# Batch 1's attention beside batch 0's second dense layer: another order of the same steps

## The chip, the cores and the metric

The kernel runs on one core of a Trainium2 chip. The metric is device time in microseconds (us) of one execution; lower is better. The engines are TensorE (PE, with PEld its weight loads), VectorE (DVE), ScalarE (ACT), GpSimd (POOL) and SyncE (SP, which here only issues transfers). Each engine works through a queue of its own in order; between engines, semaphores hold an instruction back until its inputs and its buffer are there.

## The reference

Four batches of eight heads, 768 tokens, head size 64. Attention sees the first 4 tokens (sinks) and a window of 128 tokens back; the result goes through two dense layers with a squared ReLU between them.

```python
scores = scale * np.matmul(q, k.transpose(0, 1, 3, 2))
keep = is_sink | in_window          # pos < 4, or 0 <= rel < 128
scores = np.where(keep, scores, -1000000000.0)
...
a = np.exp(scores - max); a = a / (sum(a) + 1e-09)
attn_out = np.matmul(a, v)
x = attn_out.transpose(0, 2, 1, 3).reshape(B * S, H * D)   # 3072 x 512
h = x @ w_in                                               # 512 x 2048
r = np.maximum(h, 0.0); g = r * r
out = g @ w_out                                            # 2048 x 512
```

## The kernel before

All work is cut into 992 numbered steps (`Op`), built in the code in a fixed numbering. A step is a handful of instructions on one engine: a load, a set of transposes, one pair of score tiles, one exponential, one mask, one product of a dense layer, one copy out of PSUM, one store. A batch of 768 tokens is worked on in three token blocks of 256 (s or u = 0, 1, 2). Of the heads, m counts four pairs; a score step takes two pairs in batches 1 to 3.

The order of everything is one hand-kept string, `ORDER`. `Plan.run` walks through its words. A word is a step's number, a letter for the engine where there is a choice (p, d, a, g for PE, DVE, ACT, POOL; without a letter the first engine in the step's table), and `+0` or `+1` for the pool of PSUM that it takes its buffer from. The steps are issued in that order, so the string sets, for each engine, the order of its queue, and with it the buffers: a buffer is handed on when the last reader's word has been passed, first freed, first taken:

```python
            for s in o.takes:
                if len(s.pools) > 1:
                    s.pool = s.pools[int(chosen.pop(0))]
                s.room = free[s.pool].pop(0)
            ...
            o.run(o.engine)
            for s in o.reads:
                s.readers -= 1
                if not s.readers:
                    free[s.pool].append(s.room)
```

PSUM has four such buffers of two banks: two in the pool `att`, two in `den`. Transposes, scores, values and both dense layers all take from these four, so most PE steps wait for the ACT or DVE step that empties the buffer they get.

The stages that meet in the changed stretch, with the step numbers that the text uses:

- Loads of batch 1: POOL issues q and k (37 to 44, 49 to 52; L371; 40 is the last of the first four of k, 44 the last of the first four of q), v (45 to 48, 53, 54; L380). The transfers cast to bf16. Loads of batch 2: 444 to 461 (L402, L414). 87 builds the mask constants on POOL (L257 to L259).
- Batch 0, first dense layer, third token block: products 184, 193, 187, 190 (L762, 16 matmuls of 256 columns each); their ReLU (185, 194, 188, 191; L776 on ACT, L778 on DVE) and squares (186, 195, 189, 192; L785, L787).
- Batch 0, second dense layer: first block 282 to 289 (L990) with copies 290, 291 on ACT and the store 292 (L1013); second block 297 to 308 and third 316 to 327, seven products each by sums and differences of blocks (L1239), their sums on DVE (L1213) and their copies and additions (L192, L194, L1253), stores 311 and 330 (L1282).
- Batch 1, transposes of k (200, 196, 204, 208) and q (201, 197, 205, 209) in one PE step per pair of heads (L503, four matmuls), 252 and 255 for the last two tiles; each is copied out by 198, 199, 202, 203, 206, 207, 210, 211, 253 to 257.
- Batch 1, attention: scores 216, 223 (block 0), 234, 241 (block 1), 260, 267 (block 2) on PE (L609); exponentials 217, 219, 224, 226, 235, 237, 242, 244, 261, 263, 268, 270 on ACT (L630); masks on DVE (L639, L642) or POOL (L218); sink keys 213, sink scores 214 and 258 (L568), sink values 212 (L550); values 221, 228, 239, 246, 265, 272 (L678); normalizing (L694, L695); transposes of the result, "bridges", 230, 232, 248, 250, 274, 276 (L727).
- Batch 1, first dense layer: blocks 0 and 1 together, 343 to 406, in four groups of seven products (L892) with copies `t` (L192, L194), bounded sums `r` (L942), ReLU (L967, L969) and squares (L915, L917); block 2 from 412, behind a spread copy 407 on ACT.
- Batch 2 begins: SP turns its q and k by transposing transfers (462 to 473, L460), sink keys 475, scores 485 and 478 with exponentials 486, 488, 479, 481 and masks 487, 489.
- 530 is the first product of batch 1's second dense layer.

Before the changed stretch the queues of both kernels are the same, and behind 490 they are again.

Of the kernel before, what the change touches and what calls it, by code (L numbers as in the profile page):

```python
# [18 lines left out]


ORDER = """
990 1 0 2 7 8 9 10 11 12 13 14 15 16 17 18 56d 60a 55d 991+0 3 19 57+0 61d 20 5 6 4 62+1 65 59a 67+0 58a 21 64d 89d
63a 68+0 75+1 88d 69 70 76+1 22 71+0 77 23 72 73 78 24 94a 79+1 90+0 93d 92a 95+1 80 91d 81 96a 74 100+0 82 101+0 25
26 102 83+1 97d 66 84d 27 104 85 110+1 111+0 103g 86d 152+1 112 28 113d 105d 98+0 99 153 106+0 108 114 115d 154a 116+1
118 29 160+1 109 161 162a 107 30 119 117 120+0 31 155d 163a 122 121d 123d 32 168+0 156+1 331 33 172+0 157 169 164+1
170a 165 34 35 158d 173 166a 124+1 125a 127+0 36 159d 176+1 129a 177 126d 174a 140+1 133+1 37 128d 171d 142 136 180+1
181 282+0 38 178d 167d 137d 132+0 141+1 182a 130+0 39 283 40 144 143d 41 134 42 43 332 284 285 131 145d 146+0 175a 147
135g 278 179a 286 138+1 139 287 288 148+0 150 334 151d 44 149a 279 183d 289 184+1 290 185 193+0 280 281 200+0 201 291
194 45 204+1 196+0 202 46 203 205 198a 186 197 207a 293 206 187+0 199a 216+0+0 47 48 195a 217 49 188d 234+1+0 50 235
190+0 219 208+0 87 292 237 209 295 191 218 297+0 189 220 51 336 52 212 53 210a 294 211 255+0 252+1 254 299 298 256 54  # L30
253a 257 444 223+0+1 333 238d 445 192a 226 304 213 224 221+0 312 222 300 241+1+0 301 214+0 296 244 215 302 225 446
303d 242 306 260+0+0 236 462 263 307 314 337 316+0 245d 243d 315 227 308 313 447 318 319 464 246+0 261 247 239+0 448
240 320 321 228+0 475 322d 317 229 258+0 335 259 325 449 450 310 326 230+0 451 231 452 232 248+0 233 249a 327 250 251a
323 309 305 343+1 359+1 339 338 344 467 340 345 341 360 463 329 311 453 324 328 346 465 347 361 362 363 267+1+1 348
349 350 364 268 342 365d 270 351d 366 367 375+0 352 376 377 354 368 454 355 468 356d 370 369a 357 455 391+0 456 379
264 457 262 466 458 265+0 271 393 353 459 378 269 371 392 395 358a 266 372 272+0 373 381 380 382 474 374a 397 394 273
274+0 383d 276 277 396 275a 384 469 407 386 485+0+0 388d 718 472 387 470 460 486 398 410 461 408 389 412+1 488 471
478+1+0 409 399 473 385 479 400 487 330 413 688 402 414 428+0 404 401 403 405 430 416 429 418 432 406a 489 530+0 481
415 390 417 431 419 532 689 526 411 490+0 434 420 433 435 528 421 423 491 436 437 707 482 527 422a 533 424 480 534 690
708 476+0 477 425 439 440 441 691 535 442 531 483+1 426 529 484 443a 536 494+0+0 537 438a 497 692 427 495 568+0 545  # L40
539 540 570 564 566 492 693 694 695 542 498d 501+0+0 502 565 696 541 493 571 504 697 706 538 572 698 543 569 709
517+0+1 518 546 699 573 544 547 520 700 575 503d 510+0+0 701 574 549+0 496d 583 711 576 567 577 584 578 521d 513 505
579 585 551 581 506+0 552 580 507 514 511 586 512d 553 519 713 588+0 499+0 710 500 554 702 703 555d 515+0 516 522+0
589 719 550 590 712 523 591 745+0+0 748 592 558 556 548 560 746 738+0+0 741 594d 557 593 587 595 559 562 739 561
722+0+0 747 596d 714 604+0 749d 725 597 606 599 605 600 726 601 608 607 715 508 509 723 602 524 716 525 717 656+1 657
598 720+0 658 609 620 721 659 610 622 640+0 750+0 724 611 642 612 621 641 751 613 742 603a 660 662 740 615 644 623 646
614 727+0 616 704 661 617 663 563 643 645 618 647 619 672+0 664 667 665 648 651 649 728 582 674 668 673 669 650 676
670 743+0 652 666a 675 744 653 624+1 678 671a 677 654 626 679 625 729+1+0 680 730 628 770 681 655 630 683 774+0 771
732 684 627 775 685 686 629 772 776 754+0+1 682a 755 731 631 777 687 733 773 632 734+0 735 778 635 779 757 705 761+1+0
633 637 636 781 752 758 780d 634 762 638 756 639a 736 793+0 783 789 764 790 784 759+0 737 791 785 795 760 763 782 765  # L50
794 827 828 800 832+1 766+0 786 787 767 848+0 788 850d 829 833 808 796 834 835 830 849 797 768 836 838d 810 851 753
798 837 852 812+1 792 839 853 799 854 855 856 769 801 802 804 840d 859 803 841 857 831 814 843 815 858 842a 866 844
861 805d 816 845 811 809 806 860 817 868+0 813 862 864 846 819 865 818 863 869 870 884+1 867 871 821 872 885 874 823
886d 873 875 822 847 876 916+0 824 887 888 917 889 932 825 877 878 879 890 934 820 918 880 919 920 900+1 807 902 881d
882 933 891 921 883a 901 892 904 936+0 922d 938 906 903 923 905 893 924d 895 896 907 925 894a 897 939 935 908d 927 898
928 926a 940 929 937 826 911 909 899a 913 910 930 941 931 912 942 914 943 946 915 970 955+1 944 945 957 951 974+0 948
953 971 947 952 958 975 949 959d 956 972 960 950 961 973 977+0 962 976 978 964 954 966 979d 965 963 980 968 981 982
985 967d 969 983 984 989 986 988 987
"""
# [1350 lines left out]
```

## Time and profile before

| | |
|---|---|
| median of 3 runs | 210.15 us (209.98 to 210.62) |
| profiled execution | 209.26 us, of which 207.6 us span |
| granted TensorE clock | 1.0 |
| busy: PE, PEld, DVE, ACT, POOL | 199.6, 176.2, 174.7, 133.9, 96.2 us |

The span runs from the first to the last instruction of the program. A window row shows a stretch's length, then for each engine the us in which it was busy and the number of instructions, then clock, DMA share in engines' tenths, GB/s. A timeline row shows start, length, engine, line, operation, what is written from what, and how many instructions were merged; in square brackets the idle time before it and what ended it. A matmul's shown length includes its way through the array, so PE's pace is read from start to start.

### The profile page before, as it was taken

What the parts mean: (1) busy time and instruction counts of PE and PEld (TensorE: products, weight loads), DVE (VectorE), ACT (ScalarE), POOL (GpSimd) and SP (SyncE); (2) the same over time, 40 slices, a digit from 0 to 9 for tenths busy, and PEclk for the clock granted to TensorE, in tenths of its full rate; (3) what the DMA queues carried; (4) which work ended last, traced back from release to release, by engine and by line L of the source; (5) the groups of instructions that cost most, each with busy time, mean ns of one, the idle gap of its engine ahead of it and who ended that gap; (6) DMA issues with size and microseconds to landing.
All of it is one profiled execution on the core that took longest, in us unless ns stands there. A gap on an engine that the chain in (4) does not pass through costs nothing.

```text
span 207.6 us, 6021 instructions
## 1 busy us (share of the span) xinstructions
PE 199.6 (96%) x2500; PEld 176.2 (85%) x2502; DVE 174.7 (84%) x342; ACT 133.9 (64%) x208; POOL 96.2 (46%) x137
## 2 busy tenths in 40 slices
PE   7969999999899999999999999999999999999993
PEld 7458997579878899889878988998889999999893
DVE  4387657498899998999998778999989998998853
ACT  2769458729998168898888458989871452584010
POOL 7799275699499927999333529000280000000000
PEclk9999999999999999999999999999999999999999
DMA  5999999999999999999999996901023220200205
GB/s 157 220 218 200 186 185 212 180 156 175 159 75 126 147 129 225 117 182 155 123 142 235 103 135 194 115 3 25 12 42 129 53 94 10 104 0 0 104 0 202
DMA packets 96042, 26.10 MB, mean 126 GB/s; under 512 B 86800, under 2 KB 93456, under 8 KB 96016
## 3 DMA queue, kind: packets, MB, share of 16 engines
q0 software_dynamic: 69248, 12.59, 86.5%
q1 hardware_dynamic: 25568, 12.49, 27.2%
q10 hardware_dynamic: 1200, 0.66, 1.1%
q8 instruction: 19, 0.31, 0.6%
q14 instruction: 7, 0.06, 0.1%
HBM read 27.30 MB, written 6.29 MB: 162 GB/s over the span
## 4 chain that ended last, share of the span: by engine, by line
PE 80%; DVE 6%; ACT 6%; DMA 4%; issue 2%; POOL 0%; ACTq 0%; POOLq 0%; DVEq 0%
PE py L1239 28%; PE pm L892 25%; PE pm L762 9%; PE po L678 6%; PE ps L609 4%; DMA v<-in_v_dram 4%; PE py L990 3%; ACT expm L630 2%; PE py L1100 2%; PE pt L503 1%; DVE r L942 1%; ACT gT_sb L915 1%; PE px L727 1%; DVE xn_sb L695 1%; ACT qkT L192 1%
## 5 line engine op out<-in xcount | busy, mean ns | idle before, releaser
L630 ACT ACTIVATE expm<-ps 128x1024 bf16<-128x1024 f32 (+1 forms) x48 | 43.8, 951 | 9.6 <-PE ps L609 7.6
L218 POOL TENSOR_SCALAR_AFFINE_SELECT expm<-expm 128x512 bf16<-128x512 bf16 x34 | 24.0, 740 | 42.2 <-DVE xn_sb L695 19.5
L942 DVE CUSTOM_DVE_ANT_0 r<-pm,t 128x512 bf16<-128x512 f32 x54 | 36.0, 684 | 1.6 <-PE pm L892 1.2
L1239 PEld LDWEIGHTS <-gT_sb 128*128 128x128 bf16 x320 | 30.4, 98 | 4.4 <-issue 0.6
L892 PEld LDWEIGHTS <-w_in_sb 128*128 128x128 bf16 x384 | 32.4, 114 | 1.7 <-issue 1.5
L192 ACT ACTIVATE t<-pm 128x512 f32<-128x512 f32 x42 | 24.7, 600 | 13.4 <-PE pm L892 12.7
L892 PEld LDWEIGHTS <-wi 128*128 128x128 bf16 x288 | 24.7, 114 | 0.8 <-issue 0.7
L1239 PEld LDWEIGHTS <-sg 128*128 128x128 bf16 x240 | 22.5, 98 | 3.1 <-DVE sg L1213 0.3
L192 ACT ACTIVATE osb<-py 128x256 f32<-128x256 f32 (+1 forms) x36 | 14.1, 397 | 15.7 <-PE py L1239 15.0
L762 PE MATMUL pm<-xT,w_in_sb 128*128 128x256 bf16 x192 | 22.5, 273 | 0.1
L892 PE MATMUL pm<-xs,wi 128*128 128x256 bf16 (+1 forms) x192 | 21.6, 246 | 0.0
L892 PE MATMUL pm<-xs,w_in_sb 128*128 128x256 bf16 (+1 forms) x192 | 21.5, 246 | 0.0
L762 PEld LDWEIGHTS <-w_in_sb 128*128 128x128 bf16 x192 | 20.5, 114 | 0.8 <-issue 0.5
L1239 PE MATMUL py<-wt,gT_sb 128*128 128x256 bf16 x160 | 20.7, 273 | 0.2
L1239 PE MATMUL py<-wt,sg 128*128 128x256 bf16 x160 | 20.8, 273 | 0.0
L1239 PE MATMUL py<-w_out_sb,gT_sb 128*128 128x256 bf16 x160 | 20.4, 273 | 0.0
L915 ACT ACTIVATE gT_sb<-r 128x1024 bf16<-128x1024 bf16 x17 | 18.0, 1056 | 1.8 <-DVE r L942 1.6
L678 PE MATMUL po<-v,expm 128*128 128x65 bf16 x352 | 17.9, 193 | 1.1 <-DMA v<-in_v_dram 1.1
L678 PEld LDWEIGHTS <-expm 128*128 128x128 bf16 x352 | 16.8, 97 | 2.3 <-issue 1.3
L695 DVE TENSOR_TENSOR xn_sb<-po,rc 128x512 bf16<-128x512 f32 (+1 forms) x28 | 17.2, 615 | 1.0
L1253 DVE TENSOR_TENSOR osb<-py,osb 128x256 f32<-128x256 f32 x30 | 12.1, 416 | 4.7 <-PE py L1239 4.6
L609 PE MATMUL ps<-qkT 64*128 64x128 bf16 (+1 forms) x256 | 14.5, 238 | 1.1 <-ACT expm L630 0.6
(107 smaller groups left out, 377.8 us busy)
## 6 DMA issues: line engine op xcount, KB each, us to landing
out_dram<-osb SPq DMA_DIRECT2D x11, 512.0 KB, 3.0
v<-in_v_dram POOLq DMA_DIRECT2D x24, 128.0 KB, 7.0
qn<-in_k_dram POOLq DMA_DIRECT2D x20, 128.0 KB, 6.6
qn<-in_q_dram POOLq DMA_DIRECT2D x20, 128.0 KB, 6.3
w_in_sb<-in_moe_w_in_dram POOLq DMA_DIRECT2D x4, 512.0 KB, 9.2
w_out_sb<-in_moe_w_out_dram POOLq DMA_DIRECT2D x4, 512.0 KB, 10.5
qr<-in_k_dram SPq DMA_DIRECT2D x4, 256.0 KB, 6.9
qr<-in_q_dram ACTq DMA_DIRECT2D x2, 256.0 KB, 4.2
```

The costliest lines, as they stand in the source:

```text
L192: return nc.scalar.activation(out=dst, in_=src, func=AF.Copy)
L218: nc.gpsimd.affine_select(out=e_tile, in_=e_tile, compare_op=ALU.is_ge, fill=fill, base=i - 1, pattern=[[0, n], [1 if i else -1, 128]], ch ...
L609: nc.tensor.matmul(ps[:, h2, o:o + w], lhsT=qkT_sb[r, m, 1, c, :], rhs=qkT_sb[r, m, 0, qb:qb + w // 128, :], start=(i == 0 and not biased) ...
L630: nc.scalar.activation(out=x[:, :, o:512], in_=bank_t["s", b, s, m][:, :, o:512], func=AF.Exp, scale=scale)
L678: touch(("po", b, s, m0), e, nc.tensor.matmul(pv[:, i, h2, :], lhsT=lhsT, rhs=rhs, start=(n_ == 0), stop=(n_ == len(mms) - 1)), j)
L695: touch(("po", b, s, m0), e, nc.vector.tensor_tensor(out=xn_sb[:, 2 * s:2 * s + 2, 128 * (m0 + j0):128 * (m0 + j0 + nj)].rearrange("p i (j ...
L762: nc.tensor.matmul(pm[:, i, :], lhsT=w_in_sb[:, fb // 4, kb, fb % 4:512:4], rhs=xT[:, c0 // 256:(c0 + cw) // 256, kb, :], start=(kb == 0), ...
L892: touch(tag, e, nc.tensor.matmul(y[:, bk, i, :], lhsT=weights(name, f0 + i, a), rhs=rhs[:, a, :], start=fresh and i == 0 and a == 0, stop= ...
L915: nc.scalar.activation(out=d, in_=x, func=AF.Square)
L942: touch(tag, e, nc.vector._custom_dve(TENSOR_ADD_SAT, out=d.rearrange("p n c -> p (n c)"), in0=T["y"][:, 1].rearrange("p n c -> p (n c)"), ...
L1239: touch((b, u), e, nc.tensor.matmul(region(name), lhsT=x[:, i, :], rhs=w_[:, i, :], start=first and i == 0, stop=i == HB - 1, skip_group_c ...
L1253: ins = nc.vector.tensor_tensor(out=d, in0=region(of), in1=d, op=ALU.add)
```

## The change

The word order in `ORDER` is changed between the 188th and the 476th of the 992 words. Outside that stretch the words stand where they stood. Many words gain an engine letter; for nearly all that letter names the engine which the word without it meant. 28 steps do run on another engine: 14 from DVE to ACT (copies 206, 211, 254, 257, 303, 322, 233, 365; squares 189, 353, 390, 401; ReLU 356, 388), 10 from ACT to DVE (copies 199, 207, 253, 309, 361, 367; ReLU 191; squares 192, 369, 406), masks 236 and 262 and the sink values 212 from POOL to DVE, mask 238 from DVE to POOL. In eight words the PSUM pool is another one. The start of the stretch:

```diff
-278 179a 286 138+1 139 287 288 148+0 150 334 151d 44 149a 279 183d 289 184+1 290 185 193+0 280 281 200+0 201 291
-194 45 204+1 196+0 202 46 203 205 198a 186 197 207a 293 206 187+0 199a 216+0+0 47 48 195a 217 49 188d 234+1+0 50 235
-190+0 219 208+0 87 292 237 209 295 191 218 297+0 189 220 51 336 52 212 53 210a 294 211 255+0 252+1 254 299 298 256 54
-253a 257 444 223+0+1 333 238d 445 192a 226 304 213 224 221+0 312 222 300 241+1+0 301 214+0 296 244 215 302 225 446
-303d 242 306 260+0+0 236 462 263 307 314 337 316+0 245d 243d 315 227 308 313 447 318 319 464 246+0 261 247 239+0 448
+147d 135g 278d 179a 286 138+1 139d 287 288 148+0 150 334d
+151d 44g 149a 279d 183d 289 290a 200+0 280d 291a 45g 196+0 184+0 46g 201 87g 197 212d 185a 198a 193+0 47g 48g 202d
+203d 293d 204+0 205 186d 49g 194a 187+0 295d 50g 206a 199d 207d 195a 216+0+0 217a 234+1+0 219a 237a 188d 51g 296d
+208+1 235a 209 292 336d 210a 211a 52g 53g 190+1 297+0 281d 220d 189a 255+0 213a 294d 299a 236d 191d 252+1 254a 257a
+54g 238g 298 253d 256d 444g 304 218d 192d 223+0+1 305d 462 445g 224a 214+0 215a 300 226a 221+0 446g 301a 333d 312d
+222d 241+0+1 302 242a 260+0+0 447g 313d 227d 448g 465 303a 261a 306d 244a 307 314d 308 230+0 309d 225d 310d 316+0
...
```

and its end, from batch 1's last bridges on:

```diff
-274+0 383d 276 277 396 275a 384 469 407 386 485+0+0 388d 718 472 387 470 460 486 398 410 461 408 389 412+1 488 471
-478+1+0 409 399 473 385 479 400 487 330 413 688 402 414 428+0 404 401 403 405 430 416 429 418 432 406a 489 530+0 481
...
+275a 396 398 485+0+0 386 407a 399a 486a 718g 461g 311 384d 402 388a 385d 470 400d 487d 387 389d 404a 403 405d 488a
+412+1 428+0 471 688g 429 414a 410d 408d 401a 478+1+0 689g 430a 413 409d 411d 406d 415d 479a 481a 472 416 418a 432 390a
+530+0 489d 473 330 434a 417 419 431d 420a 526d 532a 490+0 433 435 528d 421d 423 491d 436a 437d 707 482d 527d 422a 533
...
```

TensorE's queue in the stretch, by step numbers, before:

```
184 193 200 201 204 196 205 197 187 216 234 190 208 209 297 255 252 298 223 304 221 300 241 214 302 260 307 316
308 319 246 239 321 228 317 258 326 230 232 248 327 250 323 343 359 344 360 347 363 267 348 350 364 366 375 376
354 355 370 391 379 265 371 392 395 272 380 382 274 276 396 386 485 387 398 412 478 413 402 428 403 416 429 432 530
```

and after:

```
200 196 184 201 197 193 204 205 187 216 234 208 209 190 297 255 252 298 304 223 214 300 221 241 302 260 307 308
230 316 228 239 319 246 232 248 321 250 317 258 359 343 344 360 323 347 326 327 363 348 350 267 364 366 354 375
355 370 371 391 265 392 272 376 379 274 395 276 380 382 396 398 485 386 402 387 403 412 428 429 478 413 416 432 530
```

POOL issues step 87 ahead of 47 instead of behind 50, and the 16 loads 444 to 459 one after another, ahead of masks 264, 269 and 271. SP turns in the order 462, 465, 463, 464, 467, 466, 469, 468, then the store 311, where it stood behind the fourth turn before.

More of the change, by code (lines that the diff above doesn't have):

```diff
@@ L21 @@
 ORDER = """
[L22 to L26, printed above, removed]
@@ L27 @@
-181 282+0 38 178d 167d 137d 132+0 141+1 182a 130+0 39 283 40 144 143d 41 134 42 43 332 284 285 131 145d 146+0 175a 147
-135g 278 179a 286 138+1 139 287 288 148+0 150 334 151d 44 149a 279 183d 289 184+1 290 185 193+0 280 281 200+0 201 291
-194 45 204+1 196+0 202 46 203 205 198a 186 197 207a 293 206 187+0 199a 216+0+0 47 48 195a 217 49 188d 234+1+0 50 235
-190+0 219 208+0 87 292 237 209 295 191 218 297+0 189 220 51 336 52 212 53 210a 294 211 255+0 252+1 254 299 298 256 54
-253a 257 444 223+0+1 333 238d 445 192a 226 304 213 224 221+0 312 222 300 241+1+0 301 214+0 296 244 215 302 225 446
@@ L32 @@
-303d 242 306 260+0+0 236 462 263 307 314 337 316+0 245d 243d 315 227 308 313 447 318 319 464 246+0 261 247 239+0 448
[L33 to L36, printed above, removed]
@@ L37 @@
-274+0 383d 276 277 396 275a 384 469 407 386 485+0+0 388d 718 472 387 470 460 486 398 410 461 408 389 412+1 488 471
-478+1+0 409 399 473 385 479 400 487 330 413 688 402 414 428+0 404 401 403 405 430 416 429 418 432 406a 489 530+0 481
-415 390 417 431 419 532 689 526 411 490+0 434 420 433 435 528 421 423 491 436 437 707 482 527 422a 533 424 480 534 690
-708 476+0 477 425 439 440 441 691 535 442 531 483+1 426 529 484 443a 536 494+0+0 537 438a 497 692 427 495 568+0 545
-539 540 570 564 566 492 693 694 695 542 498d 501+0+0 502 565 696 541 493 571 504 697 706 538 572 698 543 569 709
@@ L42 @@
[L42 to L56, printed above, removed]
@@ L57 @@
-953 971 947 952 958 975 949 959d 956 972 960 950 961 973 977+0 962 976 978 964 954 966 979d 965 963 980 968 981 982
-985 967d 969 983 984 989 986 988 987
+990d 1d 0d 2d 7 8a 9 10a 11 12 13 14 15 16 17 18 56d 60a 55d 991+0 3g 19g 57+0 61d 20g 5g 6g 4g 62+1 65g 59a 67+0 58a
+21g 64d 89d 63a 68+0 75+1 88d 69a 70a 76+1 22g 71+0 77a 23g 72d 73 78a 24g 94a 79+1 90+0 93d 92a 95+1 80d 91d 81 96a
+74d 100+0 82d 101+0 25g 26g 102a 83+1 97d 66a 84d 27g 104a 85 110+1 111+0 103g 86d 152+1 112a 28g 113d 105d 98+0 99a
@@ new lines @@
+153 106+0 108 114a 115d 154a 116+1 118 29g 160+1 109d 161 162a 107d 30g 119d 117d 120+0 31g 155d 163a 122 121d 123d
+32g 168+0 156+1 331d 33g 172+0 157 169 164+1 170a 165 34g 35g 158d 173 166a 124+1 125a 127+0 36g 159d 176+1 129a 177
+126d 174a 140+1 133+1 37g 128d 171d 142a 136a 180+1 181 282+0 38g 178d 167d 137d 132+0 141+1 182a 130+0 39g 283 40g
+144a 143d 41g 134a 42g 43g 332d 284 285 131a 145d 146+0 175a 147d 135g 278d 179a 286 138+1 139d 287 288 148+0 150 334d
+151d 44g 149a 279d 183d 289 290a 200+0 280d 291a 45g 196+0 184+0 46g 201 87g 197 212d 185a 198a 193+0 47g 48g 202d
@@ new lines @@
+203d 293d 204+0 205 186d 49g 194a 187+0 295d 50g 206a 199d 207d 195a 216+0+0 217a 234+1+0 219a 237a 188d 51g 296d
+208+1 235a 209 292 336d 210a 211a 52g 53g 190+1 297+0 281d 220d 189a 255+0 213a 294d 299a 236d 191d 252+1 254a 257a
+54g 238g 298 253d 256d 444g 304 218d 192d 223+0+1 305d 462 445g 224a 214+0 215a 300 226a 221+0 446g 301a 333d 312d
+222d 241+0+1 302 242a 260+0+0 447g 313d 227d 448g 465 303a 261a 306d 244a 307 314d 308 230+0 309d 225d 310d 316+0
+228+1 263a 243d 318a 245d 239+0 319 320a 229d 240d 246+1 232 449g 231d 233a 450g 248+0 247d 451g 321 452g 453g 249a
@@ new lines @@
+250 338d 251a 262d 317 315d 463 464 258+1 454g 335d 467 359+1 343+1 322a 339d 345a 466 455g 456g 344 360 323 340d 341d
+347 326 259a 361d 457g 325d 337d 327 346d 363 349a 475a 362d 469 348 458g 328a 350 329d 324d 267+1+1 351d 342d 352d
+364 365a 366 354 268a 367d 375+0 459g 355 270a 264g 460g 474g 370 368d 468 371 356a 353a 372a 391+0 357d 369d 265+0
+269g 358a 377a 271g 393a 392 373d 272+0 266d 376 379 374a 274+0 273d 395 378d 381a 276 380 394d 382 277d 397a 383d
+275a 396 398 485+0+0 386 407a 399a 486a 718g 461g 311 384d 402 388a 385d 470 400d 487d 387 389d 404a 403 405d 488a
@@ new lines @@
+412+1 428+0 471 688g 429 414a 410d 408d 401a 478+1+0 689g 430a 413 409d 411d 406d 415d 479a 481a 472 416 418a 432 390a
+530+0 489d 473 330 434a 417 419 431d 420a 526d 532a 490+0 433 435 528d 421d 423 491d 436a 437d 707 482d 527d 422a 533
+424 480d 534a 690g 708 476+0 477a 425a 439 440 441a 691g 535 442d 531 483+1 426d 529d 484d 443a 536a 494+0+0 537 438a
+497a 692g 427d 495a 568+0 545d 539d 540 570a 564d 566d 492 693g 694g 695g 542a 498d 501+0+0 502a 565d 696g 541 493 571
+504a 697g 706 538d 572a 698g 543d 569 709 517+0+1 518a 546d 699g 573 544 547d 520a 700g 575 503d 510+0+0 701g 574a
@@ new lines @@
+549+0 496d 583a 711 576d 567d 577d 584d 578 521d 513a 505g 579 585d 551a 581d 506+0 552 580a 507d 514g 511a 586d 512d
+553a 519g 713 588+0 499+0 710 500d 554 702g 703g 555d 515+0 516d 522+0 589 719a 550 590a 712 523d 591d 745+0+0 748a
+592 558d 556 548d 560 746a 738+0+0 741a 594d 557d 593 587d 595 559 562d 739a 561a 722+0+0 747g 596d 714 604+0 749d
+725a 597d 606a 599 605 600 726d 601a 608 607d 715 508 509 723a 602d 524 716 525 717 656+1 657 598d 720+0 658a 609 620d
+721a 659d 610a 622d 640+0 750+0 724d 611 642a 612a 621d 641 751d 613d 742g 603a 660 662a 740g 615 644 623d 646a 614d
@@ new lines @@
+727+0 616 704g 661 617a 663 563 643d 645 618d 647 619d 672+0 664a 667 665d 648a 651 649d 728d 582 674a 668 673 669a
+650d 676 670d 743+0 652 666a 675d 744d 653a 624+1 678a 671a 677 654d 626a 679 625 729+1+0 680a 730a 628 770d 681d 655d
+630a 683 774+0 771d 732a 684 627d 775 685a 686d 629 772d 776a 754+0+1 682a 755a 731d 631 777 687d 733d 773d 632a 734+0
+735d 778a 635 779 757a 705g 761+1+0 633d 637a 636 781 752 758g 780d 634d 762a 638d 756g 639a 736 793+0 783d 789d 764a
+790d 784 759+0 737 791d 785 795a 760d 763g 782d 765g 794 827a 828d 800 832+1 766+0 786a 787d 767d 848+0 788 850d 829d
@@ new lines @@
+833 808d 796 834a 835d 830d 849 797a 768 836 838d 810d 851d 753 798 837 852 812+1 792d 839 853 799a 854a 855 856a 769
+801d 802d 804 840d 859 803 841d 857d 831d 814a 843 815 858d 842a 866d 844 861a 805d 816a 845a 811d 809d 806d 860 817
+868+0 813 862d 864d 846d 819 865d 818a 863d 869 870a 884+1 867d 871d 821d 872 885 874a 823 886d 873 875 822 847d 876a
+916+0 824a 887d 888 917 889 932d 825d 877d 878d 879 890a 934d 820d 918a 880 919d 920 900+1 807 902a 881d 882d 933d 891
+921 883a 901 892a 904 936+0 922d 938a 906a 903d 923 905 893d 924d 895 896 907 925d 894a 897a 939 935d 908d 927 898d
@@ L59 @@
+928 926a 940a 929a 937 826 911 909d 899a 913a 910d 930d 941 931d 912 942a 914d 943 946 915d 970d 955+1 944d 945d 957a
+951d 974+0 948a 953d 971d 947 952d 958 975 949d 959d 956 972d 960 950 961a 973d 977+0 962 976a 978 964d 954d 966 979d
+965 963d 980d 968d 981 982 985 967d 969 983d 984d 989 986d 988 987d
 """
```

## The prediction

> **What bounds the kernel now.** I read the page first, then busy time by stretches, the waits of TensorE, its timeline, and only then single tiles.
>
> ```profile
> PE 199.6 (96%) x2500; PEld 176.2 (85%) x2502; DVE 174.7 (84%) x342; ACT 133.9 (64%) x208; POOL 96.2 (46%) x137
> ```
>
> TensorE is busy for 96% of the span. The table below cuts out the reordered steps: from the first moved matmul (44.63 us) to the first matmul of batch 1's second dense layer (step 530, 93.11 us), after which both orders agree but for a few copies and squares.
>
> ```profile
> 44.63:51.31 6.68, 6.68 (x73) 6.47 (x72) 6.15 (x9) 4.64 (x8) 6.57 (x9) 1.00 2.78 155
> 51.31:52.94 1.63, 1.05 (x21) 0.73 (x21) 1.52 (x2) 1.63 (x3) 1.47 (x4) 1.00 1.59 299
> 52.94:74.04 21.10, 21.07 (x283) 18.17 (x281) 20.11 (x41) 14.47 (x26) 18.16 (x23) 1.00 2.08 120
> 74.04:88.25 14.21, 14.21 (x179) 13.26 (x177) 13.36 (x26) 12.04 (x19) 8.54 (x15) 1.00 1.52 157
> 88.25:89.54 1.29, 1.14 (x15) 0.89 (x14) 1.29 (x6) 1.29 (x3) 1.29 (x3) 1.00 1.12 253
> 89.54:93.11 3.57, 3.57 (x59) 3.40 (x57) 3.53 (x8) 3.47 (x8) 3.57 (x5) 1.00 1.65 161
> sum 48.48, PE 47.73 PEld 42.92 DVE 45.96 ACT 37.54 POOL 39.60; mean PE 7.95 PEld 7.15 DVE 7.66 ACT 6.26 POOL 6.60
> ```
>
> Columns: length, then busy us of PE, PEld, DVE, ACT, POOL, then clock, DMA, GB/s. Of 48.48 us PE shows only 0.75 idle. DVE is nearly as full (45.96); ACT has 10.9 us free. So a new order has little to win here and much to lose. PE's two longest waits in the stretch:
>
> ```profile
> PE ps L609 <- ACT expm L630: 0.6, 1, 0.6
> PE pm L892 <- ACT expm L630: 0.2, 1, 0.2
> ```
>
> Short waits hide inside busy time, so I look at starts.
>
> ```profile
> 43.77 1.03 PE L990 MATMUL py<-w_out_sb,gT_sb 128*128 128x512 bf16 x4
> 44.63 3.66 PE L762 MATMUL pm<-xT,w_in_sb 128*128 128x256 bf16 x32
> 48.13 1.50 PE L503 MATMUL pt<-ident,qn 128*128 128x128 bf16 x24
> 49.47 1.91 PE L762 MATMUL pm<-xT,w_in_sb 128*128 128x256 bf16 x16
> 51.31 0.73 PE L609 MATMUL ps<-qkT 64*128 64x256 bf16 x14
> 52.61 0.40 PE L609 MATMUL ps<-qkT 64*128 64x128 bf16 x6 [0.58 <-ACT expm L630]
> ```
>
> From start to start, 32 matmuls of 256 columns take 48.13 - 44.63 = 3.50 us (0.109 each) and 24 of 128 columns 1.34 us (0.056 each). By these unit prices the end of the stretch hides three more waits:
>
> ```profile
> 85.78 0.71 PE L727 MATMUL px<-ident,xn_sb 128*128 128x128 bf16 x8
> 86.33 0.60 PE L892 MATMUL pm<-xs,w_in_sb 128*128 128x256 bf16 x4
> 86.82 0.60 PE L892 MATMUL pm<-xT,wi 128*128 128x256 bf16 x4
> 87.35 0.50 PE L609 MATMUL ps<-qkT 64*128 64x256 bf16 x8
> 87.78 0.63 PE L892 MATMUL pm<-xs,w_in_sb 128*128 128x256 bf16 x4
> 88.25 0.60 PE L892 MATMUL pm<-xs,wi 128*128 128x256 bf16 x4
> 89.00 0.61 PE L892 MATMUL pm<-xd,w_in_sb 128*128 128x128 bf16 x8 [0.15 <-ACT expm L630]
> ```
>
> Between 85.78 and 86.33 it is 0.55 for eight transposes worth 0.45 (0.10 lost); between 86.33 and 86.82 0.49 for 0.44 (0.05); between 88.25 and 89.00 0.75 for 0.44 (0.31). With the 0.58 ahead of 52.61, that is 1.04 us: the most that any order of the same matmuls can win.
>
> **The change part by part.** No instruction is added or removed. Some 280 steps move, 28 change engine, and PSUM banks pass on differently.
>
> *Keys before the first dense layer.* Now 32 matmuls of batch 0's third token block (184, 193) come first, then batch 1's transposes (200, 201, 204, 196, 205, 197). After: 200, 196, 184, 201, 197, 193, 204, 205, 187. From 44.63: 200 and 196 (4 x 0.056 each) end at 45.07, 184 (16 x 0.109) at 46.82. There 201 wants the last of batch 1's four q loads, step 44:
>
> ```profile
> L371 POOL DMA_DIRECT2D qn<-in_q_dram x1: 891/891/891, 40.7 to 40.7; - x1
> DMA to landing us min/median/max: 7.0/7.0/7.0
> ```
>
> Issued at 40.66, it lands at 47.66. POOL's queue is the same up to step 46, so it lands no earlier after the change. Now 201 comes at 48.35 (third group of transposes) and does not notice; after, PE waits 47.66 - 46.82 plus some 0.04 to start = **0.88 us**. PE executes in order: 197, 193 and all else stand behind it. Next late would be 204's bank, but its copies 202 and 203 on DVE are done by 49.6 even in the worst case below, and 204 comes at 49.89.
>
> *Something could move that landing.* The store of batch 0's first rows (512 KB, step 292) waits for the second ACT copy (291). That copy now runs behind a relu; after, it runs right behind 290, at about 44.9, and the store leaves near 45.5 instead of 48.18.
>
> ```profile
> 47.56 0.60 ACT L192 ACTIVATE osb<-py 128x512 f32<-128x512 f32 x1
> 48.18 0.36 SPq L1013 DMA_DIRECT2D out_dram<-osb  x1
> L380 POOL DMA_DIRECT2D v<-in_v_dram x4: 873/874/876, 41.6 to 44.5; - x4
> DMA to landing us min/median/max: 7.1/7.1/7.2
> ```
>
> The four v loads issued from 41.6 to 44.5 land from 48.7 to 51.6, all in the 3 us after the store's issue, and take 7.1 us like the load before them. So a store beside loads cost at most 0.2: bounds 0.88 to 1.1; I take 0.88. The Trainium skill, page "DMA: Bandwidth & Descriptors", section "Queues, rings and completion order", says that each DMA engine takes turns packet by packet between the queues that have work; by it the load's remaining 2.16 us at 45.5 would double. By that rule, the trace disagrees: its loads kept their 7 us.
>
> *Scores 216 and 234* stay neighbours, and 234's second half still uses the bank that 216's first exponential (217) frees. PE reaches 216 at 52.17 and ACT, done with square 195 at 52.5, finishes 217 at 53.46: the **0.58** stays.
>
> *Second dense layer beside the scores (297 to 317).* I added PE's groups one after another from 53.83 and set each beside the ACT or DVE instruction that frees its bank or gives its input, the ACT ones by the mean times below, each starting 0.1 before its forerunner ends.
>
> ```profile
> 66.62 1.45 PE po L678 x48
> L630 ACT ACTIVATE expm<-ps 128x1024 bf16<-128x1024 f32 x8 | 8.0, 1028 | 0.3 <-POOL expm L218 0.2
> ```
>
> The first row, of the chain that ended last, gives value matmuls 0.030 each. Entering 64-row matmuls costs 0.1 (86.82 + 0.44 = 87.26, next start 87.35), a group of eight then lasts 0.43, one of twelve 0.56, with 0.04 more behind it. Stations: 297 at 56.05, 223 at 59.66, 241 at 61.74, 260 at 63.34, 316 at 65.93, 246 at 68.9, 317 at 71.1. Most have 0.3 us or more. One hasn't: 316 takes the bank that exponential 244 frees. ACT runs 242, 303, 261, 244 (exponentials of 1.03, a copy of 0.39) from 62.55 to 66.0; PE is there at 65.93: **0.10**.
>
> *Batch 1's first dense layer (359 to 432).* PE reaches 359 at 72.36, 267 at 78.58 and 398 at 87.65 without a wait, since the three hidden waits above go (412 no longer stands right behind 485). Two come instead. 428's bank hangs on DVE: 400, mask 487 and 389 end at 90.95, PE comes at 90.85: **0.15** with the start. 530's bank is freed by exponential 479, the last of nine ACT instructions without a gap from 88.3 (399, 486, 388, 404, 488, 414, 401, 430, 479):
>
> ```profile
> L192 ACT ACTIVATE t<-pm 128x512 f32<-128x512 f32 x12 | 7.3, 606 | 1.4 <-PE pm L892 1.1 <-ACT expm L630 0.2
> L630 ACT ACTIVATE expm<-ps 128x768 bf16<-128x768 f32 x7 | 5.5, 807 | 0.0
> L915 ACT ACTIVATE gT_sb<-r 128x1024 bf16<-128x1024 bf16 x4 | 4.2, 1053 | 0.3 <-DVE r L942 0.2
> L917 DVE TENSOR_TENSOR gT_sb<-r 128x1024 bf16<-128x1024 bf16 x3 | 2.1, 686 | 0.0
> L550 POOL TENSOR_TENSOR vs<-vs_in,head_rows 32x130 bf16<-32x130 f32 x12 | 4.8, 400 | 0.7
> L694 DVE RECIPROCAL rc<-po 128x8 f32<-128x8 f32 x6 | 1.2, 204 | 0.0
> ```
>
> Five of about 0.6, three exponentials of 0.8 and square 401 of 1.05 (moved here from DVE, 0.69), each overlapping the next by 0.1, end at 93.95. PE comes at 93.77: **0.22**.
>
> *Engines.* 14 steps go DVE to ACT, 10 ACT to DVE, two masks POOL to DVE, one back, and batch 1's sink values (212, four instructions) POOL to DVE. ACT gains 9.9 - 7.6 = 2.2 us and has 10.9 free, so only the place above counts. DVE saves 0.7 without 212. That step is not shown on DVE: four times 0.20 (DVE's small reciprocal) to 0.40 (POOL's own), 0.8 to 1.6; I take 1.2. It lies in the wait for 201; without that cover it would push 207, which 216 needs, to within 0.1 of PE.
>
> *POOL and SP.* The mask constants (87) pass four loads and the 16 loads of batch 2 lose the masks between them; they run in one row from about 57.9. Their transposing turns on SP come earlier, and the store 311 goes behind eight of them, to about 77; its buffer is next wanted at about 95. Sink keys 475 on ACT find their turn done by 65. Nobody waits: nothing.
>
> *Sum.* After: 0.88 + 0.58 + 0.10 + 0.15 + 0.22 = 1.93; before 1.04; difference **+0.89 us**. Behind 530 PE has hardly a gap to give it back. The profiled execution, 209.26 us (span 207.6 and 1.66 around it), becomes 210.15; it is 0.89 below the median of the runs, so the median 210.15 becomes **211.0**.
>
> **The rivals.**
> *The load is there (faster).* If step 44's load took 6.1 us or less instead of 7.0, 201 would not wait. For it: such loads spread widely.
>
> ```profile
> L371 POOL DMA_DIRECT2D qn<-in_q_dram x6: 873/873/891, 33.4 to 50.0; - x6
> DMA to landing us min/median/max: 3.3/6.3/11.7
> ```
>
> Against it: the load's whole queue ahead of it is unchanged. Without 0.88 the sum is 1.05 against 1.04; if the two bank waits at the end are absent too because DVE and ACT got ahead, it is -0.46 or so: 209.7. Half of this case's chance passes the bound of 0.3%. It decides at a landing by 46.8.
> *The waits cancel.* At the median landing, 6.3, 201 waits 0.2 and the rest balances: 210.3.
> *ACT becomes the bound before 530.* If the spread (407, 1.06 us) or one square more falls into the row of nine, 530 waits 0.95 longer: 212.0. For it: ACT gains 2.2 us here; against it: 10.9 free.
> *The store halves the loads.* 201's load lands 2.16 later: 213.2. Against it: the 7.1 above. The Trainium skill, page "DMA: Bandwidth & Descriptors", section "Queues, rings and completion order", would have it so.
>
> **How the numbers follow.** Forecast 0.52 (its own range 210.4 to 211.6), load there 0.11, cancel 0.19, ACT 0.13, store 0.05. About 0.3%, 0.63 us, is what a measurement can tell from no change. Slower: 0.52 less 0.05 for its low end, plus 0.13 and 0.05 = 0.65; same: 0.05 + 0.19 + half of 0.11, less rounding = 0.28; faster 0.07. The range 209.8 to 212.4 leaves out most of the store case and half of the faster one.
>
> **What would show it.** A wait of TensorE for the q load, in a row of transposes (L503) near 47 us, of about 0.9; a wait of 0.6 for the exponential near 53; no gap behind 88.25's successor, but short ones before the first matmul of L1239 at about 94.0, against 93.11. If L503 shows no wait on a DMA, step one of the sum is wrong; if 530 starts later than 94.6, the ACT row is.

## Result and profile after

| | before | after |
|---|---|---|
| median | 210.06 us of 8 runs | 211.52 us of 8 runs |
| ratio | | 1.0074, interval 1.0049 to 1.0099 |
| profiled execution | 209.26 us, span 207.6 | 211.37 us, span 209.6 |
| stretch, first moved matmul to step 530 | 48.48 us (44.63 to 93.11) | 50.15 us (44.91 to 95.06) |
| from step 530 to the last matmul's start | 110.89 us | 111.01 us |

The changed kernel is slower, by 1.5 us. In the two traces the span grew by 2.0: 1.67 in the stretch, 0.12 behind it, the rest ahead of it. That last part isn't the change's: the queues up to the stretch are the same, and in the runs below with the same queues it begins anywhere from 44.3 to 45.7 us. Stretches are therefore compared, and only then spans. Each stretch comes from one trace, so a difference of a few tenths between two runs counts only where single waits account for it.

The first lines answer to the busy times and the stretch table of before; the lines of the program stand 4 higher than there (L892 is now L896). The page of the changed kernel:

```profile
PE 199.7 (95%) x2500; PEld 175.5 (84%) x2502; DVE 177.9 (85%) x343; ACT 135.5 (65%) x212; POOL 94.2 (45%) x131
```

Its stretches (length, then busy us of PE, PEld, DVE, ACT, POOL):

```profile
44.91:53.35 8.44, 7.57 (x87) 7.03 (x86) 8.09 (x16) 5.62 (x9) 6.80 (x8) 1.00 2.19 188
53.35:75.60 22.25, 21.56 (x286) 18.36 (x285) 22.01 (x40) 15.98 (x28) 19.64 (x23) 1.00 1.89 114
75.60:95.06 19.46, 19.25 (x245) 17.41 (x246) 18.59 (x36) 17.13 (x28) 9.73 (x17) 1.00 1.68 164
sum 50.15, PE 48.38 PEld 42.79 DVE 48.70 ACT 38.73 POOL 36.17; mean PE 16.13 PEld 14.26 DVE 16.23 ACT 12.91 POOL 12.06
```

DVE's busy time is 3.2 us longer in the whole span, 2.7 in the stretch, although the prediction had it save 0.7 and pay 1.2 for the sink values (212). From 53.35 to 75.60 it is busy in 22.01 of 22.25 us. TensorE's waits in the stretch:

```profile
PE ps L613 <- ACT expm L634: 0.6, 1, 0.6
PE pm L896 <- DVE xs L858: 0.4, 1, 0.4
PE pt L507 <- DMA qn<-in_q_dram: 0.3, 1, 0.3
PE ps L613 <- DVE xn_sb L699: 0.3, 1, 0.3
PE pm L896 <- DVE r L946: 0.2, 1, 0.2
```

Three of the five name DVE; before, neither of PE's two did. Their places in PE's timeline:

```profile
47.10 0.33 PE L507 MATMUL pt<-ident,qn 128*128 128x128 bf16 x3
47.73 0.45 PE L507 MATMUL pt<-ident,qn 128*128 128x128 bf16 x5 [0.30 <-DMA qn<-in_q_dram]
...
62.23 1.05 PE L1243 MATMUL py<-wt,sg 128*128 128x256 bf16 x8
63.57 0.62 PE L613 MATMUL ps<-qkT 64*128 64x128 bf16 x12 [0.28 <-DVE xn_sb L699]
...
74.16 1.04 PE L1243 MATMUL py<-w_out_sb,gT_sb 128*128 128x256 bf16 x8
75.61 0.63 PE L896 MATMUL pm<-xs,wi 128*128 128x256 bf16 x4 [0.40 <-DVE xs L858]
...
90.39 0.60 PE L896 MATMUL pm<-xs,w_in_sb 128*128 128x256 bf16 x4
91.16 0.60 PE L896 MATMUL pm<-xs,w_in_sb 128*128 128x256 bf16 x4 [0.18 <-DVE r L946]
91.60 1.72 PE L896 MATMUL pm<-xd,w_in_sb 128*128 128x128 bf16 x24
93.25 0.50 PE L613 MATMUL ps<-qkT 64*128 64x256 bf16 x8
```

By starts and the prediction's unit prices the losses are: step 201, 47.73 - 47.10 less three transposes, 0.46; score 260, 1.34 less 0.97, about 0.35 with rounding; product 347, 1.45 less 0.87, 0.57; product 403, 0.77 less 0.44, 0.34; product 428 in the row of 24, 0.19. With the 0.58 of 234 and a few of about 0.1 they make 2.75 us. Before had 1.04; the difference, 1.71, is the stretch's 1.67.

Why was DVE late? Its timeline ahead of 347, with POOL's beside it (second fence, also of the changed kernel):

```profile
70.71 0.68 DVE L825 TENSOR_TENSOR w_in_sb<-w_in_sb 128x1024 bf16<-128x1024 bf16 x1
71.31 1.12 DVE L646 TENSOR_TENSOR expm<-expm,tri 128x1024 bf16<-128x1024 bf16 x1
72.35 1.12 DVE L1217 TENSOR_TENSOR sg<-gT_sb,sg 128x1024 bf16<-128x1024 bf16 x1
73.39 1.11 DVE L815 TENSOR_TENSOR wi<-w_in_sb,wi 128x1024 bf16<-128x1024 bf16 x1
74.43 0.41 DVE L858 TENSOR_TENSOR xs<-xT 128x512 bf16<-128x512 bf16 x1
74.94 0.60 DVE L858 TENSOR_TENSOR xs<-xT,xs 128x512 bf16<-128x512 bf16 x1
75.47 0.62 DVE L858 TENSOR_TENSOR xs<-xT 128x512 bf16<-128x512 bf16 x1
```

```profile
71.96 2.00 POOL L222 TENSOR_SCALAR_AFFINE_SELECT expm<-expm 128x512 bf16<-128x512 bf16 x2
73.91 0.91 POOL L418 DMA_DIRECT2D v<-in_v_dram  x1
74.84 1.97 POOL L554 TENSOR_TENSOR vs<-vs_in,head_rows 32x130 bf16<-32x130 f32 x4
```

The same kind of operation takes 0.68 in the first row and 1.11 to 1.12 in the next three, around POOL's mask 264. The last two rows, of 0.60 and 0.62, stand beside POOL's sink values (74.84), where such a step takes 0.41 alone. The pair of sum and mask repeats 17 us earlier, with DVE's mask 220 and sum 294 beside POOL's mask 238 (DVE's and POOL's timelines of the changed kernel):

```profile
54.50 1.22 DVE L1035 TENSOR_TENSOR wt<-w_out_sb,wt 128x2048 bf16<-128x2048 bf16 x1
55.64 0.99 DVE L643 TENSOR_TENSOR expm<-expm,mask 128x768 bf16<-128x768 bf16 x1
56.55 1.12 DVE L1217 TENSOR_TENSOR gT_sb<-gT_sb 128x1024 bf16<-128x1024 bf16 x1
57.59 0.68 DVE L646 TENSOR_TENSOR expm<-expm,tri 128x1024 bf16<-128x1024 bf16 x1
```

```profile
55.00 2.12 POOL L222 TENSOR_SCALAR_AFFINE_SELECT expm<-expm 128x512 bf16<-128x512 bf16 x2 [3.29 <-ACT expm L634]
```

Before had the same meeting once in full, at mask 236 (POOL's and DVE's timelines of before):

```profile
59.97 1.22 POOL L218 TENSOR_SCALAR_AFFINE_SELECT expm<-expm 128x512 bf16<-128x512 bf16 x2
```

```profile
60.63 1.10 DVE L1213 TENSOR_TENSOR sg<-gT_sb,sg 128x1024 bf16<-128x1024 bf16 x1
```

There the mask kept the time that another has with no mask or sum of DVE's beside it (1.21 at 79.21), and DVE's sum took 1.10. So the price stood in the trace from which the prediction was made. Added up over the stretch, DVE's rows are longer than alone by some 2.8 us in after and 0.6 in before. These 2.2, with 1.2 for the sink values and the 0.7 saved, are the 2.7 by which DVE's busy time grew.

### The profile page after: what moved, and what is told of

Same layout as the page of the kernel before. It is cut to its first block, busy times and chain, and to the rows that moved or that the text cites. A ratio compares the mean times of both kernels' runs of the same rounds, so it can differ in the third digit from the quotient of the medians.

```text
span 209.6 us, 6022 instructions
## 1 busy us (share of the span) xinstructions
PE 199.7 (95%) x2500; PEld 175.5 (84%) x2502; DVE 177.9 (85%) x343; ACT 135.5 (65%) x212; POOL 94.2 (45%) x131
## 4 chain that ended last, share of the span: by engine, by line
PE 58%; DMA 18%; DVE 12%; ACT 5%; POOL 3%; issue 2%; SPq 0%; ACTq 0%; POOLq 0%; DVEq 0%
PE py L1243 24%; PE pm L896 23%; DMA qn<-in_k_dram 6%; DMA w_out_sb<-in_moe_w_out_dram 6%; DMA qn<-in_q_dram 3%; PE po L682 3%; PE ps L613 3%; DMA vs_in<-in_v_dram 2%; PE pm L766 2%; PE py L1104 2%; DVE sg L1217 2%; ACT gT_sb L919 2%; POOL w_in_sb L311 1%; DVE xn_sb L699 1%; DVE r L946 1%
## 5 line engine op out<-in xcount | busy, mean ns | idle before, releaser
L896 PEld LDWEIGHTS <-w_in_sb 128*128 128x128 bf16 x384 | 32.4, 114 | 1.8 <-issue 1.4
L196 ACT ACTIVATE t<-pm 128x512 f32<-128x512 f32 x41 | 23.8, 599 | 15.6 <-PE pm L896 14.3
L896 PEld LDWEIGHTS <-wi 128*128 128x128 bf16 x288 | 24.5, 114 | 1.6 <-issue 0.9
L896 PE MATMUL pm<-xs,wi 128*128 128x256 bf16 (+1 forms) x192 | 21.7, 246 | 0.4 <-DVE xs L858 0.4
L896 PE MATMUL pm<-xs,w_in_sb 128*128 128x256 bf16 (+1 forms) x192 | 21.5, 246 | 0.2 <-DVE r L946 0.2
L919 ACT ACTIVATE gT_sb<-r 128x1024 bf16<-128x1024 bf16 x18 | 19.1, 1059 | 1.9 <-DVE r L946 1.8
L682 PEld LDWEIGHTS <-expm 128*128 128x128 bf16 x352 | 16.7, 97 | 2.3 <-issue 1.2
```

Of the source, the lines that this page charges most:

```text
L196: return nc.scalar.activation(out=dst, in_=src, func=AF.Copy)
L682: touch(("po", b, s, m0), e, nc.tensor.matmul(pv[:, i, h2, :], lhsT=lhsT, rhs=rhs, start=(n_ == 0), stop=(n_ == len(mms) - 1)), j)
L896: touch(tag, e, nc.tensor.matmul(y[:, bk, i, :], lhsT=weights(name, f0 + i, a), rhs=rhs[:, a, :], start=fresh and i == 0 and a == 0, stop= ...
L919: nc.scalar.activation(out=d, in_=x, func=AF.Square)
```

## Experiments

| run | stretch, us | ratio to before, interval |
|---|---|---|
| a1_load_in_time | 50.11 | 1.0079, 1.0056 to 1.0102 |
| b1_early_transposes | 49.35 | 1.0053, 1.0028 to 1.0078 |
| a2_masks_on_dve | 49.93 | 1.0082, 1.0058 to 1.0106 |
| a3_old_engines | 55.24 | 1.0297, 1.0278 to 1.0315 |
| c2_dve_relief | 49.14 | 1.0058, 1.0037 to 1.0079 |
| c3_chain | 50.61 | 1.0105, 1.0084 to 1.0127 |
| c5_relief_chain | 49.93 | 1.0072, 1.0048 to 1.0096 |
| c4_start_of_before | 48.64 | 1.0036, 1.0010 to 1.0062 |
| d1_relief_and_start | 48.32 | 1.0008, 0.9983 to 1.0034 |
| d2_relief_start_400 | 48.64 | 1.0032, 1.0002 to 1.0063 |
| d3_190_between_scores | 48.41 | 1.0052, 1.0023 to 1.0081 |
| d4_190_and_square | 48.07 | 1.0031, 1.0004 to 1.0059 |

Where intervals overlap, the reading rests on the stretch and on single waits. Of the expectations below, d1's theory came out; the times of a1 and b1 lay near theirs, for reasons that are partly others; a2 and c2 lay between theory and rival; c4, c5, d2 and d4 were slower than their theories, and a3, c3 and d3 slower than the rival too.

**The early transposes.** In the first run 201 and 197 go behind product 193, late enough for the load:

```diff
 200+0 280d 291a 45g 196+0 184+0 46g
-201 87g 197 212d 185a 198a 193+0
+87g 212d 185a 198a 193+0 201 197
```

> The kernel after, with the two q transposes 201 and 197 behind product 193, so that their load has landed when TensorE comes. Theory M (from the trace after): TensorE lost 0.46 us on the late load, 0.35 and 0.57 on DVE results (normalizing 222 ahead of scores 260, sum 340 ahead of product 347) and 0.34 and 0.19 on DVE chains ahead of 403 and 428; DVE ran from 52.2 to 75 us almost without a gap and can start only 0.28 earlier, so of the 0.46 some 0.28 come back: 211.2 us, and the waits ahead of 260 and 347 grow a little. The prediction's reading (the late load is the cost and passes whole to the end): 0.88 back, 210.6 us.

The load's wait went, and the stretch stayed:

```profile
48.82 0.55 PE L507 MATMUL pt<-ident,qn 128*128 128x128 bf16 x7
49.67 0.61 PE L507 MATMUL pt<-ident,qn 128*128 128x128 bf16 x8 [0.29 <-DVE qkT L198]
```

From 48.82 to 49.67 seven transposes worth 0.39 take 0.85: 0.46 again, now for a bank that 201's own copy on DVE frees for 204. The other waits kept their sizes (0.35, 0.56, 0.34, 0.19). So taking the load's wait away gains nothing by itself; a copy stands right behind it. The reverse, before with only its first nine PE steps in the new order:

```diff
-184+1 290 185 193+0 280 281 200+0 201 291 194 45 204+1 196+0 202 46 203 205 198a 186 197
+200+0 290 280 196+0 281 184+0 201 291 45 197 202 46 185 198a 193+0 203 194 204+0 205 186
```

> The kernel before with only its first nine TensorE steps in the new order (200 196 184 201 197 193 204 205 187), and the copies that belong to them. Theory M: 201's last matmul waits 0.5 to 0.7 for the load, nothing gives it back or adds to it: 210.5 to 210.8 us. The prediction's price, 0.88: 210.9 us. If the load is not the cost: 210.1 us.

The new start alone cost 0.87 us: 0.50 at 47.60 for the load, and 234's wait grew from 0.6 to 0.9, which its theory did not have. Only the first part is one of after's losses; there 234's wait stayed at 0.58.

**Which engine does what.** Masks 238 and 264 on DVE take away what POOL does beside DVE:

```diff
-238g ... 264g
+238d ... 264d
```

> The kernel after, with masks 238 and 264 on DVE instead of POOL. Theory M: masks 220 and 262, sums 294 and 315 and the weight sum 335 took 0.99 to 1.12 us on DVE instead of 0.55 to 0.68 because POOL's masks worked on SBUF at the same time; without them DVE saves 2.2 us, pays 1.4 for the two masks, the wait ahead of 347 (0.57) goes and that ahead of 260 (0.35) shrinks: 210.7 to 211.1 us, the sums at 0.68 us. Rival: DVE is simply full, and two more masks cost it 1.4 us: 211.9 us or more.

DVE's timeline in that run:

```profile
71.22 0.68 DVE L646 TENSOR_TENSOR expm<-expm,tri 128x1024 bf16<-128x1024 bf16 x1
71.82 0.69 DVE L1217 TENSOR_TENSOR sg<-gT_sb,sg 128x1024 bf16<-128x1024 bf16 x1
72.42 0.68 DVE L815 TENSOR_TENSOR wi<-w_in_sb,wi 128x1024 bf16<-128x1024 bf16 x1
```

Each operation is back at its own time and 347 no longer waits, so the lengthening of these three is shown to come from POOL's mask. The kernel gained little (the stretch 0.22 us, the median nothing): DVE had the masks to do itself, and product 371, at 82.60, started 0.86 late. It is the longer of these two waits:

```profile
PE pm L896 <- DVE r L946: 0.9, 2, 0.7
```

With all 28 engine changes undone, in the new order:

> The kernel after with the engine of each of the 28 changed steps as before: the new order alone. Rival E (the engine moves are the cost): 210.5 us, only the late load's 0.46 above before. Theory M: the order sets which DVE and POOL steps meet, and the late load stays; with three masks and the sink values back on POOL they meet elsewhere: 211.0 to 212.0 us.

The stretch is 5.1 us longer than after's, and the time some 4 us above both expectations. TensorE's listed waits there add up to 5.8 us, of which 4.4 are for DVE; two of the largest:

```profile
PE pm L896 <- DVE t L198: 1.3, 1, 1.3
PE po L682 <- DVE r L946: 0.9, 1, 0.9
```

So the engine changes taken together are not the loss: in this order they save 5.1 us. That clears no single one of them, mask 238 on POOL least of all. Next, a smaller edit: sink values 212 back on POOL behind the last v load, mask 264 on DVE right behind 262, POOL's sink values 474 later.

```diff
-212d ... 54g 238g ... 262d 317 ... 264g 460g 474g ... 271g 393a
+54g 212g 238g ... 262d 264d 317 ... 460g ... 271g 474g 393a
```

> The kernel after with less for DVE and POOL to meet over: sink values 212 back on POOL, where it was idle (behind load 54); mask 264 on DVE right behind 262 (in the kernel with 264 late in DVE's queue TensorE waited 0.86 us ahead of product 371); batch 2's sink values 474 behind mask 271. Theory M: 262, 315 and 335 take 0.68, the waits ahead of 347 (0.57) and 371 go, that ahead of 260 stays, since mask 238 still slows 220 and 294: 0.6 less than after, a ratio to before of 1.0045. Rival (DVE is full, any relief comes back as another wait): 1.007 to 1.008.

347's wait went and none came for it: the stretch is 1.01 shorter than after's. Of this 0.57 are 347's; 0.39 are the load's wait, which was 0.07 because this run came to the stretch 0.3 later. The intervals of the two ratios overlap, and the sink values 474 and 212 moved in the same run, so 347's gain is not the mask's alone.

**The chain ahead of 403.** Copy 383, sum 384, square 385 and sum 400 stand one behind the other on DVE, in the timeline of after:

```profile
88.36 0.69 DVE L198 COPY t<-pm 128x512 f32<-128x512 f32 x1 [0.29 <-ACT xT L196]
89.09 0.69 DVE L946 CUSTOM_DVE_ANT_0 r<-pm,t 128x512 bf16<-128x512 f32 x1
89.82 0.69 DVE L921 TENSOR_TENSOR gT_sb<-r 128x1024 bf16<-128x1024 bf16 x1
90.43 0.68 DVE L946 CUSTOM_DVE_ANT_0 r<-pm,t 128x512 bf16<-128x512 f32 x1
```

384 needs 383's copy and 385 needs 384's result: 0.73 from start to start. 400 needs neither and follows after 0.61; it ends at 91.11, and 403 starts at 91.16. The next run takes 400 ahead of the square, and 389 ahead of a mask:

```diff
-385d 470 400d 487d 387 389d
+400d 385d 470 387 389d 487d
```

> The kernel after with two swaps in DVE's queue near 90 us: bounded sum 400 ahead of square 385, and 389 ahead of mask 487. Theory M: the waits ahead of products 403 (0.34) and 428 (0.19) go and nothing behind takes their place: 0.5 less than after, a ratio to before of 1.005. Rival (ACT sets the pace there, as the prediction had it for 530): step 530 waits for exponential 479 instead and the ratio stays 1.007.

403's wait went, 428's stayed, and a new one came ahead of 530, where the prediction had put it. (347's wait was 0.80 in this trace, 0.23 more than in after, with nothing changed near it.)

```profile
94.14 1.34 PE L896 MATMUL pm<-xs,wi 128*128 128x128 bf16 x16
95.56 0.71 PE L1243 MATMUL py<-w_out_sb,gT_sb 128*128 128x256 bf16 x5
```

16 matmuls worth 0.90 take 1.42: 0.52 for buffers that ACT's row ahead of 530 frees; ReLU 388 in it had waited 0.23 for square 385. In after the same 16 take 0.89. Relief and chain together did not add up either:

> Both edits, DVE's relief and the two swaps. Theory M: the waits are apart in time, so the gains add: 1.1 less than after, a ratio to before of 1.002. Rival: they don't add, 1.005.

There the load's wait was 0.74 and 0.54 stood ahead of 530. d2 (below) shows that the swap of 400 alone costs as much as both swaps: 48.64 us, as in c4. There it cost 0.64 ahead of 428.

**The old start.** The run before this, with all words up to score 216 as they were before:

> As the kernel with relief and swaps, and besides with all words up to scores 216 in the order of before, so that products 184 and 193 come ahead of batch 1's transposes and the q load has landed. Theory M: 0.46 for the load and up to 0.3 more ahead of 234 come back: 1.6 to 1.9 less than after, a ratio to before of 0.998 to 1.0. Rival (DVE takes it back, as when the load's wait turned into one for a bank): 1.002, as without this edit.

Against c5 the stretch fell by 1.29: the load's wait (0.74) and 260's (0.35) are gone. So those 0.35 us too belong to the words up to 216. The likely link is weight sum 281. In the new order it stands in DVE's row at 54.50 (1.22 us, shown above), ahead of the normalizing that 260 waits for; with the old start it is done earlier, and that normalizing begins 16.7 us behind the stretch's start, in after 17.9. No run moved 281 alone. Then the same without the swaps, and with 400's swap alone:

> After, with the relief of DVE (212 and mask 264 off their places, sink values 474 later) and all words up to 216 in the order of before, but without the two swaps (400 ahead of 385, 389 ahead of mask 487). Theory (the swaps cost as much as they save: they turned 0.34 + 0.19 us ahead of 403 and 428 into 0.18 + 0.28 + 0.25 ahead of 428 and 530): waits of TensorE left are 0.58 (exponential 217), 0.34 (403), 0.19 (428), 1.1 us against before's 1.04, so a ratio of about 1.000 (0.999 to 1.002). Rival (the swaps were right and the rest of the loss lies outside the counted waits): not below the 1.0036 of the run with the swaps.

> As the run beside it, with one of the two swaps: bounded sum 400 runs ahead of square 385 on DVE. Theory (403 waits for the chain 383, 384, 385, 400 on DVE): the 0.34 ahead of 403 goes and 402's and 403's buffers come earlier, ratio 0.0015 below the run beside it. Rival (square 385 and with it ReLU 388 on ACT then come later and push ACT's row of nine): a wait of 0.2 to 0.3 ahead of 530 or just before it at about 94, ratio equal to the run beside it.

The first came out as its theory had it: 48.32 us, 0.16 less than before's stretch, and no change of the time that can be measured. Left are 234's 0.58, 0.25 ahead of 403 and 0.19 ahead of 428. In the second 403's wait went and 428 waited 0.64; its rival named the right kind of price in the wrong place.

**234's wait.** From d1, product 190 moves between the two scores, its ReLU 191 to ACT, copies 210 and 211 to DVE; the last run also puts square 189 on DVE:

```diff
-217a 234+1+0 219a 237a 188d 51g 296d 208+1 235a 209 292 336d 210a 211a 52g 53g 190+1 297+0 220d 189a ...
+217a 190+0 219a 188d 191a 234+0+1 51g 296d 208+0 235a 209 237a 292 336d 52g 53g 297+0 220d 210d 211d 189a ...
```

> As the first run, with product 190 (16 matmuls, 1.75 us) between scores 216 and 234 in a buffer that is long free (206's), its ReLU 191 on ACT behind exponential 219, copies 210 and 211 on DVE. Theory (234's 0.58 us is the wait for exponential 217 alone, and only because nothing stands between the two): the 0.58 goes, no wait above 0.1 replaces it before 298, ratio 0.0025 below the first run, that is about 0.9975. Rival (ACT's four exponentials come later by as much as PE gains): transposes 255 and 252 or scores 223 wait 0.3 to 0.6 for exponential 235 or copy 211, ratio as the first run.

> As the run with product 190 between the scores, with square 189 on DVE (0.68 us, behind copies 210 and 211) instead of ACT (1.07), where it stood ahead of copies 254 and 257. Theory (scores 223 waited 0.33 us because ACT, pushed back by the late exponentials, reached copies 254 and 257 late): that wait falls to 0.1 or less, 0.17 stays ahead of product 297, and the stretch from the first product 184 to the first matmul of 530 takes 48.0 us or less, where the kernel before takes 48.48 and the one with relief and the old start 48.32; ratio 0.997 to 1.000. Rival (DVE has no room for 0.68 more): a new wait of 0.3 or more for DVE's copies, sums or masks between 57 and 66 us, stretch at 48.3 or more.

In d3 the 0.58 went; 0.17 came ahead of 297 and 0.33 ahead of 223, for ACT's copy of 255 and 252: the rival. Its ratio, 1.0052, is not explained by that: the stretch is as long as before's, and of the 1.2 us by which its trace's span is longer 1.05 lie ahead of the stretch. With the square off ACT only the 0.17 stayed, and the stretch is the shortest of all. Row by stretch of the last run:

```profile
44.95:93.02 48.07, 47.95 (x618) 42.83 (x617) 46.42 (x87) 38.02 (x63) 34.99 (x48) 1.00 1.94 147
```

That is 0.41 less than before, and still the ratio is above 1: 1.0031, barely clear of no change. Its trace, of an execution of 210.57 us, shows a loss 37 us behind the stretch:

```profile
130.47 0.40 PE L571 MATMUL pk<-qkT,kblk 128*32 128x512 bf16 x4 [1.22 <-DMA qkT<-qn]
```

Batch 3's sink scores wait for the last of SP's transposing transfers (SP's timeline and the time to landing of this transfer, first of the last run, then of before):

```profile
126.33 1.20 SPq L463 DMA_TRANSPOSE qkT<-qn  x1
DMA to landing us min/median/max: 4.0/4.0/4.0
```

```profile
125.22 1.20 SPq L460 DMA_TRANSPOSE qkT<-qn  x1
DMA to landing us min/median/max: 2.4/2.4/2.4
```

It went out 1.1 later than before's, although the stretch ended 0.1 earlier, and took 1.6 longer to land. The late issue by itself accounts for little: in c4 the same transfer went out even later, at 127.08, landed after 2.4, and the wait was 0.27. Of all the traces only this one and d2's, which waited 1.16 here, show 4.0; the others show 2.4. From step 530 to the last matmul the run takes 112.29 us against 110.89. Why that transfer takes 4.0 us in two traces was not found, nor how many of d4's executions have it. A stretch won here can be lost there. None of the twelve kernels is measurably faster than the one before.

## Why the prediction was right or wrong

The direction was right, and the time lay inside the range: 211.0 forecast, 211.52 measured. The sum under it, +0.89 forecast and +1.71 counted, was right only in parts, and in part the agreement is luck. With the measured sizes of the sum's own terms (0.46 for the load, 0.58 for 234, 0.19 for 428) against the 1.04 of before, only +0.19 is left, which would have been no change that can be told. What made the kernel slower is mostly DVE's waits, which no term had.

- *The load, 0.88: measured 0.46.* PE came to 201 as worked out, 2.19 after the stretch's start, and the load landed at 47.69 (forecast 47.66). Two parts of it were mis-sized. Three of 201's four transposes need earlier loads and ran at 47.10; only the fourth waited (0.17). And this execution reached the stretch 0.28 later with the load landing at the same time (0.25): in c5, which reached it at 44.58, the wait was 0.74, in c2, at 45.21, it was 0.07. The first run above also shows that a copy stands behind the load: without the load's wait the same 0.46 stay.
- *234's 0.58: stays*, measured 0.58. Two runs show that it is no floor: 190 in between takes it away, for 0.17 elsewhere.
- *316's 0.10: did not occur*; PE came later, after the waits ahead of it.
- *428's 0.15: measured 0.19*, for DVE's sum 389 as said.
- *530's 0.22: did not occur in after.* PE was held up ahead of it, at 403 and 428. Where 403's wait was taken away (c3, c5), waits of 0.5 appeared before 530. The place was right, but only behind a wait that the prediction did not have.
- *Before's three hidden waits (0.46 together) go: right.*
- *The step that failed is "Engines": that DVE saves 0.7 us and only ACT's row before 530 counts.* DVE's waits at 260, 347 and 403 are 0.35, 0.57 and 0.34, together 1.26 us that no term had. Every duration was taken from a row of before and held fixed, while the moves put POOL's masks beside DVE's sums. 347 is this (a2, c2), and the trace of before had such a row (60.63). 260 belongs to the words up to 216 (c4), most likely through sum 281. 403 is the place of 400 in DVE's row, behind a square that could wait and two steps that depend on each other (0.73 and not 0.6).
- *212 on DVE, estimated at 1.2: measured 1.17.*
- *The store.* SP's timeline of after has it, and the load of step 44, issued at 40.49, has this time to landing:

```profile
45.73 0.36 SPq L1017 DMA_DIRECT2D out_dram<-osb  x1
DMA to landing us min/median/max: 7.2/7.2/7.2
```

  The load took 7.2 us instead of 7.0, with 2 us of it beside the store. In the eight traces with the early store it took 7.0 to 7.3, in the six with the late one 6.7 to 7.1, so the 0.2 is hardly clear of the spread. The rival that halves the loads, 2 us more, did not happen.
- *ACT as the bound before 530*: not in after; its first sign is c3.
- *The rival with the load there early* has a slip: without the two bank waits at the end (0.15 and 0.22) its sum is 0.36 below before's, not 0.46.

The load's term was too large by 0.42, 316 and 530 by 0.32, DVE's were too small by 1.26, and small gaps made 0.3: from 0.89 to 1.71 within the rounding.

## What to carry over

Where TensorE loses only 1 us of 48, as here, a new order mostly moves waits: price the second thing that stands ready behind each wait before counting its removal as a gain. An engine as full as DVE here (46 of 48 us) needs its durations checked for what will run beside it after the change, not only added up; look in the trace of before for a row where the two already met. And compare stretches by a landmark, so that a loss 40 us later, at another deadline, is not taken for the change's own.
